# Seam between a long convolution and a GLU: last turns read from PSUM, first output in channel parts, seven residual additions as accumulating DMAs

## The chip, the cores and the metric

The kernel runs on one core of a Trainium2 chip. The metric is the device time of one execution in microseconds, the median of the runs. An execution's profile has a span, from its first to its last instruction, which is a little shorter than its time. All times below are microseconds unless they are marked ns. The engines are PE (TensorE), DVE (VectorE), ACT (ScalarE), POOL (GpSimd) and SP (SyncE, which issues most DMAs).

## The reference

One sequence of S = 2048 rows and D = 448 channels goes through two residual blocks, both modulated by a condition vector `c`.

```python
mod = (silu(c) @ w_mod).reshape(1, 6, 1, -1)
sa, ca, ga, sb, cb, gb = ...                      # six vectors of 448
h = layernorm(x) * (1 + ca) + sa
x = x + ga * A(h, k, v, shift_k, ssm_k, ssm_D)    # convolution block
h = layernorm(x) * (1 + cb) + sb
x = x + gb * B(h, w_gate, w_up, w_down)           # GLU block

def A(q, k, v, ...):
    kv = causal_depthwise_conv(k, shift_k, 4 taps) * v
    y  = causal_depthwise_conv(kv, ssm_k, S taps)  # by FFT of length 2S
    return q * (y + kv * ssm_D)

def B(x, w_gate, w_up, w_down):                   # F = 1792
    return (sigmoid(x @ w_gate) * (x @ w_up)) @ w_down
```

## The kernel before

**The convolution.** The long convolution is done as a transform by matmuls. Channels are split into two halves `h` of C = 224. `ak[h]` and `av[h]` (128 partitions x 32 x 224) hold the transforms of the filter and of `kv`. Between two transform stages a 32x32 turn is needed. It is made either on DVE, in place, for 28 channels at a time (`turn`, L181 to L183), or by a bounce through DRAM (`half_out`, `eight_out`, `half_in`, L336 to L345).

`stage2_v` (L306 to L325) loops over p = 8h + n, 16 iterations. In each, PE transforms a block of `av` (tile `s2v`, L316), DVE multiplies it by the filter (tile `m`, L320), and one iteration later `stage2_back` (L327 to L334) has PE transform it back (tile `sa`, L333) and ACT copy it from PSUM to `av` (L334). After each iteration the function `beside` (L664 to L704) adds the work of other parts that is to stand there: turns by the table `TURNS` (L660), the second transform of the filter (`stage2_k`, PE and an ACT copy, tag "y"), the modulation vectors (`mod_load` on SP, `mod_parts` and `mod_sum` on PE with an ACT copy behind each), loads, the statistics of the first layer norm, the gates (`gates`, L454: ACT and POOL prepare `gt[h, i]`), and for p from 12 on one output of the first half.

**The outputs and gates.** `stage_out(h, i)` (L347) transforms four row tiles (of 16) and one channel half to the final `y`: 16 matmuls of 224 columns into a PSUM tile (L354). `y_copy` (L357) has ACT copy it to SBUF. `gate` (L363) multiplies the prepared `gt[h, i]` by `y` (L367) and adds the product to the residual `x1` (L368). The gates of half 0 run on POOL, beside the last four iterations. Those of half 1 run on DVE: (1,0) straight from PSUM behind the loop, (1,1) to (1,3) from ACT's copies, later.

**The seam** (L706 to L725 and L903 to L924). Behind the loop come the last turn (n = 7 of half 1), the high parts of the first GLU weights (`plain_hi`, ACT) and the low remainders (`plain_lo`, DVE), modulation 5 (the gate vector of the GLU, `gbrow`), the outputs of half 1, modulation 3 (shift of the second norm, in `cols`), and the statistics of the second norm for row tiles 0 to 3 (`ln2_stats`: one tile on ACT, three on DVE; `ln2_end`: two roots on ACT, reciprocal and product on DVE). `norm_rows` (L750) normalises four row tiles into `xn`; `dup` (L758) copies 64 channels twice side by side, so that a turned tile holds them in both halves of the partitions; `norm_turn` (L765) turns them by PE into PSUM; `norm_full` (L774) has ACT apply scale and shift into `full`.

**The GLU.** All matmuls of the GLU take operands of type float32r (fp32r in the profile). Each operand is a rounded high part and a low remainder. The operand tiles of the first four "plain" quarters are "B11", "B21" (row tiles 0 to 3) and "B12", "B22" (4 to 7). `plain_half(p, q, n, f)` (L937) does 22 matmuls into tile `gu` (L944) for a weight group q, row group n and half f; the order of its 11 terms is in `OPS` or `LATE`. Then come a sigmoid (ACT, L948), a product (DVE, L949) and the split of the result (`finish_h`, L860). `down` (L873) multiplies the result by `w_down` (tile `d`, L884), and DVE adds it to `x1` (L887). The lists `turns` and `ends` (L971 to L979) say which work stands inside and behind each `plain_half`. `turn_full` (L926) makes "B12" and "B22"; it stands inside the quarter with p = 1, f = 1, its two calls after 11 and after 22 matmuls. From L1144 on 12 steps follow, of another multiplication scheme, with their side jobs in `jobs` (L1136).

**What sets the order.** The order of instructions on each engine's queue is the order in the text: `tc.manual_schedule()` (L520) keeps it. Each engine takes its own queue in that order and waits by semaphores. PSUM has 8 banks: tag "t" has two buffers of two banks, "y" and "sa" have one of two banks each; a new tile of a tag waits until the last reader of the old one is done. DMAs are issued by SP and ACT; POOL issues none.

Of the kernel before, what the change touches and what calls it, by code (L numbers as in the profile page):

```python
# [10 lines left out]
F32 = mybir.dt.float32  # L11
F32R = mybir.dt.float32r
# [67 lines left out]
def adaln_conv_glu_kernel(ctx: ExitStack, tc: tile.TileContext, q, kT, v, ssm, shift, dskip,  # L80
# [224 lines left out]

    def stage2_v(between):  # L306

        for h in range(2):
            for n in range(8):
                x, k = block(av[h], h, n), block(ak[h], h, n)  # L310
                pts = [two("t", f"s2v{h}_{n}_{b}") for b in range(2)]
                for ex in range(2):
                    for b in range(2):
                        for r in (0, 64):
                            c = r ^ 64 * b
                            PE.matmul(pts[b][c:c + 64, ex, :D], w2[r:r + 64, ex], x[r:r + 64, b], start=True, stop=True)  # L316
                m = [pairs(quad("m", 4, f"m{h}_{n}_{b}")) for b in range(2)]
                w = DT if eights(h, n) else 28
                for b in range(2):
                    DVE.tensor_mul(cols4(m[b], h, n), cols4(rows(pts[b]), h, n), k[:, b].unsqueeze(1).to_broadcast([P, 2, D // w, w]))  # L320
                products.append((h, n, m))
                if len(products) == 2:
                    stage2_back()
                between(h, n)
        stage2_back()  # L325

    def stage2_back():  # L327
        h, n, m = products.pop(0)
        pt = two("sa", f"sa{h}_{n}")
        for b in range(2):  # L330
            for ex in range(2):
                r = slice(64 * ex, 64 * ex + 64)
                PE.matmul(pt[r, b, :D], wa[:, b, r], m[b][:, ex], start=True, stop=True)  # L333
        ACT.activation(block(av[h], h, n), cols4(rows(pt), h, n), AF.Copy)  # L334
# [11 lines left out]

    def stage_out(h, i, tag):  # L347

        pt = two(tag, f"y{h}_{i}")
        for b in range(2):  # L350
            for jj in range(2):
                g = 4 * i + 2 * b + jj
                for s in range(2):
                    PE.matmul(pt[64 * s:64 * s + 64, b, jj * C:jj * C + C], wb[:, 16 * s + g], av[h][:, 16 * s + g], start=True, stop=True)  # L354
        return rows(pt)
# [7 lines left out]
    def gate(h, i, y, eng):  # L363

        gg = gt[h, i]
        xs = late["x1"][:, 4 * i:4 * i + 4, h * C:(h + 1) * C]
        eng.tensor_mul(pairs(gg), pairs(gg), y)  # L367
        eng.tensor_add(xs, xs, gg)  # L368

# [145 lines left out]

    def plain_lo(q, t):
        x = plain(q, t)
        DVE.tensor_sub(x[:, 1], ring["raw"][:, t], x[:, 0])

# [135 lines left out]
    for n in range(2):  # L655
# [5 lines left out]
             7: ((1, 4),), 8: ((1, 5),), 9: ((0, 4), (0, 5)), 10: ((0, 6), (0, 7)), 11: ((1, 6),), 12: ((1, 7),), 13: ((1, 4),),  # L661
             14: ((1, 5),), 15: ((1, 6),)}

    def beside(h, n):  # L664

        p = 8 * h + n
        for at in TURNS.get(p, ()):
            turn(av[at[0]], at[1])
        for m in {0: (0,), 1: (1,), 3: (2,), 12: (4,)}.get(p, ()):
            mod_sum(m)  # L670
        if 4 <= p < 12:
            stage2_k(1, p - 4)
        if p in (0, 2, 11):
            mod_parts({0: 1, 2: 2, 11: 4}[p], "y")
        if p == 4:
# [49 lines left out]
    y1.append(stage_out(1, 3, "sa"))  # L725
# [24 lines left out]
    def norm_rows(n, rows_=range(4)):  # L750
        for i in rows_:
            g = slice(4 * n + i, 4 * n + i + 1)
            if n == 0:
                DVE.tensor_scalar(xn[:, i], x1[:, i], rstd2[:, g], nmr2[:, g], op0=OP.mult, op1=OP.add)
            else:
                ACT.activation(xn[:, i], x1[:, 4 * n + i], AF.Identity, bias=nmr2[:, g], scale=rstd2[:, g])

    def dup():  # L758
        x = xn[:, :, P:P + 64]
        DVE.tensor_copy(xd.rearrange("p a (r c) -> p a r c", r=2), x.unsqueeze(2).to_broadcast([P, 4, 2, 64]))  # L760

# [140 lines left out]

    yc = [y_copy(1, 1, y1[1])]  # L903
# [8 lines left out]
    for t in range(2):  # L912
        norm_full(0, t, pts[0][:, t])
    for t in range(2):
        DVE.tensor_copy(xf["B11"][:, t], full[:, t])  # L915
    x_lo("B11")
    for t in range(2):
        norm_full(0, 2 + t, pts[1][:, t], xf["B21"][:, t])
    for t in range(2):
        norm_full(0, 2 + t, pts[1][:, t])  # L920
    x_lo("B21")
    ln2_stats(4, 5, 6, 7, act=(4,))
    split_plain(1, 2, 3)
# [10 lines left out]
    OPS = ((2, 0, 0, 0), (2, 1, 0, 0), (3, 0, 0, 1), (3, 1, 0, 1), (2, 0, 0, 2), (0, 0, 1, 0), (0, 1, 1, 0), (0, 0, 1, 2), (1, 0, 1, 1), (1, 1, 1, 1), (1, 0, 1, 3))  # L934
    LATE = ((2, 0, 0, 0), (2, 1, 0, 0), (3, 0, 0, 1), (3, 1, 0, 1), (0, 0, 1, 0), (0, 1, 1, 0), (1, 0, 1, 1), (1, 1, 1, 1), (2, 0, 0, 2), (0, 0, 1, 2), (1, 0, 1, 3))

    def plain_half(p, q, n, f, between=None):  # L937
        xs_ = (("B11", "B21"), ("B12", "B22"))[n]
        pt = two("t", f"gu{q}_{n}_{f}")
        ops = [(m, g) for m in range(11) for g in range(2)] if f == 0 and n == 0 else [(m, g) for g in range(2) for m in range(11)]  # L940
        order = LATE if p == f == 0 else OPS
        for i, (m, g) in enumerate(ops):
            t, s, b, k = order[m]
            PE.matmul(pt[:, g], plain(q, t)[:, s, g, f * P:f * P + P], xf[xs_[b]][:, k], start=m == 0, stop=m == 10, skip_group_check=True)  # L944
            if i in (10, 21) and between:
                between(i > 10)
# [17 lines left out]
    def form(i, k):  # L964
# [34 lines left out]
    def step(i, h, jobs):  # L999
# [131 lines left out]
        if first:  # L1131
# [3 lines left out]

    jobs = {0: {"0": [do(w_form, "A12", 4), do(w_form, "A22", 5), do(load_gu, 3, 0, 2)], "a": [do(w_form, "S4", 6)]},  # L1136
            1: {"b": [do(stats_end, 2, 3)], "c": [do(norm_rows, 2)], "e": [dup], "f": [do(turn_of, 2, 0, 1, tag="t")]},
            2: {"f": [do(turn_of, 2, 2, 3, tag="t")], "h": [do(norm_rows, 3, (0, 1))]},
            3: {"a": [do(norm_rows, 3, (2, 3))], "b": [dup], "f": [do(turn_of, 3, 0, 1, tag="t")]},
            4: {"a": [do(x_hi, "B11")], "b": [do(x_lo, "B11"), do(turn_of, 3, 2, 3)], "c": [do(t_sums, 1, 2)], "d": [do(t_sums, 3)], "e": [do(x_hi, "T2")],  # L1140
# [59 lines left out]
```

## Time and profile before

| | |
|---|---|
| median of 3 runs | 582.17 (581.55 to 583.97) |
| the profiled execution | 581.7 |
| its span | 579.9 |
| instructions | 7739 |
| PE busy | 547.4 (94% of the span) |
| DVE busy | 446.2 (77%) |
| ACT busy | 285.5 (49%) |
| POOL busy | 63.8 (11%) |
| DMA traffic | 107.72 MB, mean 186 GB/s |
| mean granted TensorE clock | 0.994 |

Busy time is the time in which an engine executes something; where PE is busy, its matmuls are pipelined and their ends are modelled. In timelines a line has the start, the time it took, the engine, the line of the kernel, the operation, output and inputs, the shape and the number of instructions merged, and in brackets the engine's idle time before it with what ended it. A view by stages has for each stretch of time the busy time of each engine (with the number of instructions), the granted clock of PE (1.00 is full), the share of the DMA engines and GB/s.

### The profile page before, as it was taken

What the parts mean: (1) busy time and instruction counts of PE and PEld (TensorE: products, weight loads), DVE (VectorE), ACT (ScalarE), POOL (GpSimd) and SP (SyncE); (2) the same over time, 40 slices, a digit from 0 to 9 for tenths busy, and PEclk for the clock granted to TensorE, in tenths of its full rate; (3) what the DMA queues carried; (4) which work ended last, traced back from release to release, by engine and by line L of the source; (5) the groups of instructions that cost most, each with busy time, mean ns of one, the idle gap of its engine ahead of it and who ended that gap; (6) DMA issues with size and microseconds to landing.
All of it is one profiled execution on the core that took longest, in us unless ns stands there. A gap on an engine that the chain in (4) does not pass through costs nothing.

```text
span 579.9 us, 7739 instructions
## 1 busy us (share of the span) xinstructions
PE 547.4 (94%) x2988; PEld 414.8 (72%) x2988; DVE 446.2 (77%) x526; ACT 285.5 (49%) x487; POOL 63.8 (11%) x54
## 2 busy tenths in 40 slices
PE   7997897899889999998999999999999999999997
PEld 6564432224457888876788888888888888888886
DVE  0899798997887868889989889886565556878564
ACT  4899495985458677346536453443121212333220
POOL 1000006978810000000000000000000000000000
PEclk9999998999989999999999999999999999999999
DMA  8999699897730224659748467567454563120103
GB/s 279 248 258 399 195 228 238 257 231 203 144 105 2 82 78 167 250 226 341 265 193 289 169 232 256 197 251 264 158 189 146 173 217 137 73 101 0 64 0 127
DMA packets 46552, 107.72 MB, mean 186 GB/s; under 512 B 19762, under 2 KB 24884, under 8 KB 45492
## 3 DMA queue, kind: packets, MB, share of 16 engines
q1 hardware_dynamic: 40212, 82.46, 47.2%
q10 hardware_dynamic: 6304, 24.78, 10.8%
q8 instruction: 23, 0.38, 0.3%
q14 instruction: 13, 0.11, 0.1%
HBM read 70.92 MB, written 35.78 MB: 184 GB/s over the span
## 4 chain that ended last, share of the span: by engine, by line
PE 75%; ACT 8%; DMA 8%; DVE 5%; issue 2%; SPq 2%; DVEq 0%; ACTq 0%
PE d L884 22%; PE b L853 15%; PE a L853 10%; PE c L853 9%; PE gu L944 6%; DMA ak<-kdk 3%; PE sa L333 2%; PE s2v L316 2%; PE y L354 2%; PE s2k L285 2%; DMA kdk<-ak 1%; SPq L195 1%; DMA inb<-in_wgu_dram 1%; DMA inb<-in_ssm_dram 1%; PE pt L771 1%
## 5 line engine op out<-in xcount | busy, mean ns | idle before, releaser
L884 PE MATMUL d<-wd,h 128*128 128x448 f32 x672 | 145.6, 366 | 2.1 <-DVE x L887 1.4
L884 PEld LDWEIGHTS d<-wd,h 128*128 128x128 f32 x672 | 125.8, 188 | 15.6 <-DVE x L887 1.8
L853 PE MATMUL b<-xt,ring 128*128 128x512 f32 x408 | 99.6, 392 | 1.1 <-DVE st L1067 0.9
L853 PEld LDWEIGHTS b<-xt,ring 128*128 128x128 f32 x408 | 76.1, 188 | 16.5 <-issue 1.3
L887 DVE TENSOR_TENSOR x<-x,d 128x896 f32<-128x896 f32 (+1 forms) x57 | 60.7, 1068 | 19.2 <-PE d L884 19.1
L853 PE MATMUL a<-x,ring 128*128 128x512 f32 x264 | 63.8, 389 | 0.0
L853 PEld LDWEIGHTS a<-x,ring 128*128 128x128 f32 x264 | 49.6, 188 | 10.3
L862 ACT ACTIVATE h<-st 128x512 fp32r<-128x512 f32 x56 | 35.2, 629 | 33.0 <-DVE st L871 20.6
L868 ACT ACTIVATE st<-st 128x512 f32<-128x512 f32 x24 | 15.2, 633 | 73.1 <-DVE st L1109 42.2
L865 DVE TENSOR_TENSOR h<-st,h 128x512 fp32r<-128x512 f32 x56 | 38.5, 688 | 15.1 <-ACT h L862 15.1
L183 DVE STREAM_TRANSPOSE av<-av 128x896 f32<-128x896 f32 x24 | 44.6, 1888 | 4.9 <-ACT av L334 2.6
L944 PE MATMUL gu<-x,ring 128*128 128x512 f32 x176 | 42.0, 392 | 0.8 <-DVE x L915 0.5
L1088 ACT ACTIVATE st<-st 128x512 f32<-128x512 f32 x12 | 7.6, 632 | 68.1 <-DVE st L1087 68.1
L320 DVE TENSOR_TENSOR m<-s2v,ak 128x896 f32<-128x896 f32 x32 | 33.4, 1089 | 7.1 <-PE s2v L316 4.1
L944 PEld LDWEIGHTS gu<-x,ring 128*128 128x128 f32 x176 | 32.7, 188 | 8.4 <-DVE x L915 0.7
L834 ACT ACTIVATE ring<-sum 128x512 fp32r<-128x512 f32 x28 | 17.3, 626 | 36.0 <-DVE sum L815 19.2
L853 PE MATMUL c<-x,ring 128*128 128x512 f32 x144 | 34.7, 390 | 0.0
L316 PE MATMUL s2v<-av,w 64*64 64x448 f32 x256 | 32.3, 558 | 0.7 <-DVE av L183 0.5
L853 PEld LDWEIGHTS c<-x,ring 128*128 128x128 f32 x144 | 27.0, 188 | 5.2
L333 PE MATMUL sa<-m,wa 128*64 128x448 f32 x128 | 27.5, 551 | 2.6 <-ACT av L334 2.6
L853 PE MATMUL c<-xt,ring 128*128 128x512 f32 x120 | 29.1, 389 | 0.0
L871 DVE TENSOR_TENSOR st<-st 128x512 f32<-128x512 f32 x24 | 16.6, 691 | 12.5 <-ACT st L868 12.4
(161 smaller groups left out, 780.7 us busy)
## 6 DMA issues: line engine op xcount, KB each, us to landing
fd<-ring ACTq DMA_DIRECT2D x35, 512.0 KB, 3.7
ring<-fd SPq DMA_DIRECT2D x35, 512.0 KB, 3.4
wdk<-wd ACTq DMA_DIRECT2D x7, 896.0 KB, 3.6
wd<-wdk SPq DMA_DIRECT2D x7, 896.0 KB, 4.5
inb<-in_wgu_dram SPq DMA_DIRECT2D x6, 1024.0 KB, 6.0
kdk<-ak SPq DMA_DIRECT2D x4, 896.0 KB, 9.9
x<-in_q_dram SPq DMA_DIRECT2D x4, 896.0 KB, 12.5
ak<-kdk SPq DMA_DIRECT2D x4, 896.0 KB, 16.7
```

The source lines that it names most:

```text
L183: DVE.transpose(x, x)
L316: PE.matmul(pts[b][c:c + 64, ex, :D], w2[r:r + 64, ex], x[r:r + 64, b], start=True, stop=True)
L320: DVE.tensor_mul(cols4(m[b], h, n), cols4(rows(pts[b]), h, n), k[:, b].unsqueeze(1).to_broadcast([P, 2, D // w, w]))
L333: PE.matmul(pt[r, b, :D], wa[:, b, r], m[b][:, ex], start=True, stop=True)
L834: ACT.activation(forms[name, i][:, 0], w_src(name), AF.Copy)
L853: PE.matmul(pt, wh(s, t), x[:, k], start=start and m == 0, stop=stop and m == len(ops) - 1, skip_group_check=True)
L862: ACT.activation(hh, h, AF.Copy)
L865: DVE.tensor_sub(hl, h, hh)
L871: DVE.tensor_mul(y[:, 0], y[:, 0], y[:, 1])
L884: PE.matmul(pt[:, i, :D], h[:, (2 * e + i) * P:(2 * e + i + 1) * P], x, start=m == 0, stop=m == len(ops) - 1)
L887: DVE.tensor_add(y, y, rows(pt)[:, a:b])
L944: PE.matmul(pt[:, g], plain(q, t)[:, s, g, f * P:f * P + P], xf[xs_[b]][:, k], start=m == 0, stop=m == 10, skip_group_check=True)
```

## The change

1. **Last two blocks of `stage2_back` (h = 1, n = 6 and 7).** PE writes the block into PSUM with 28 channels in every 32, and DVE's transpose reads PSUM and writes `av`. ACT's copy and the turn in place go. For n = 7 the PSUM tile has tag "t".
2. **Modulations and first-half outputs earlier.** `mod_parts(4)` at p = 10, `mod_sum(4)`, `mod_load(5)` and the first of the four outputs of half 0 at p = 11, `mod_parts(5)` at p = 14 (tag "y" for "sa"), `mod_sum(5)` at p = 15.
3. **First GLU weights.** `mod_load(3)`, three of the four `plain_hi` and their `plain_lo` stand ahead of the last `stage2_back`; these `plain_lo` are on POOL. `gate_wd(0)` is on DVE.
4. **Output (1,0) in two channel parts**, 196 and 28 of 224 columns, each with its own PSUM tile; the gate and the add are split likewise.
5. **Residual additions.** Of the eight gates only (1,0) adds on an engine. The other seven issue from POOL a DMA that adds `gt` to `x1`.
6. **Second norm, row tiles 0 to 3.** ACT's copy of y(1,1) stands between the two roots. Three rows are normalised on DVE, one on ACT. The duplicate copy goes; the tile of 64 channels is turned by four transposes and four matmuls with the identity. DVE writes the first two high parts straight from PSUM; their copy in `full` is made later by ACT.
7. **Behind it.** Weights 0 and 1 of group q = 1 are split before the statistics of row tiles 4 to 7. `norm_rows(1)` and `dup` stand behind the first half of the first quarter instead of its second, with the odd rows on DVE; the first turns of row group 1 stand inside p = 1, f = 0. Orders of terms change (`LATE`, `OPS1`), and more first halves interleave gate and up.
8. **Late duplicates** of row groups 2 and 3 are on ACT instead of DVE. The space for POOL's DMA descriptors is 2048 instead of 1024.

```diff
-    def stage2_v(between):
+    def stage2_v(between, last):
...
+        last()
         stage2_back()
...
     def stage2_back():
         h, n, m = products.pop(0)
-        pt = two("sa", f"sa{h}_{n}")
+        straight = h and n > 5
+        pt = two("t" if h and n == 7 else "sa", f"sa{h}_{n}")
...
-                PE.matmul(pt[r, b, :D], wa[:, b, r], m[b][:, ex], start=True, stop=True)
+                y = pt[r, b, :D] if not straight else pt[r, b].rearrange("p (j c) -> p j c", c=32)[:, :, :28]
+                PE.matmul(y, wa[:, b, r], m[b][:, ex], start=True, stop=True)
+        if straight:
+            y = pt.rearrange("p b (j c) -> p (b j) c", c=32)[:, :, :28]
+            DVE.transpose(av[h][:, :, 28 * n:28 * n + 28].rearrange("q p c -> q c p"), y.rearrange("q p c -> q c p"))
+            return
...
-        eng.tensor_add(xs, xs, gg)
+        if (h, i) == (1, 0):
+            eng.tensor_add(xs, xs, gg)
+        else:
+            POOL.dma_start(xs, gg, accum_op=OP.add)
...
-    def ln2_end(i0, n_act=2):
+    def ln2_end(i0, n_act=2, between=None):
         for i, j, w in ((i0, i0 + n_act, 1.0 / D), (i0 + n_act, i0 + 4, 1.0)):
+            if i > i0 and between:
+                between()
...
-        for m in {0: (0,), 1: (1,), 3: (2,), 12: (4,)}.get(p, ()):
+        for m in {0: (0,), 1: (1,), 3: (2,), 11: (4,), 15: (5,)}.get(p, ()):
             mod_sum(m)
...
-        if p in (0, 2, 11):
-            mod_parts({0: 1, 2: 2, 11: 4}[p], "y")
+        if p in (0, 2, 10):
+            mod_parts({0: 1, 2: 2, 10: 4}[p], "y")
...
-        if p == 12:
+        if p == 11:
             mod_load(5)
...
-        if p >= 12:
-            gate(0, p - 12, y_copy(0, p - 12, stage_out(0, p - 12, "y")), POOL)
-
-    stage2_v(beside)
-    mod_load(3)
-    turn(av[1], 7)
-    ring["k1"] = big.tile([P, 7168], F32R, tag="k1", name="ring")
-    for t in (2, 3, 0, 1):
-        plain_hi(0, t)
-    mod_parts(5, "sa")
-    y1 = [stage_out(1, 0, "t")]
-    mod_sum(5)
-    gate_wd(0)
-    for t in (2, 3, 0, 1):
-        plain_lo(0, t)
-    gate(1, 0, y1[0], DVE)
-    y1.append(stage_out(1, 1, "t"))
+        if 11 <= p < 15:
+            gate(0, p - 11, y_copy(0, p - 11, stage_out(0, p - 11, "y")), POOL)
+        if p == 14:
+            mod_parts(5, "y")
+
+    def first_forms():
+        mod_load(3)
+        ring["k1"] = big.tile([P, 7168], F32R, tag="k1", name="ring")
+        for t in (2, 0, 1):
+            plain_hi(0, t)
+        for t in (2, 0, 1):
+            plain_lo(0, t, POOL)
+
+    stage2_v(beside, first_forms)
+    plain_hi(0, 3)
+    parts = slice(0, 7 * 28), slice(7 * 28, C)
+    y10 = [stage_out(1, 0, "t", parts[0])]
+    mod_parts(3, "sa")
+    gate_wd(0, DVE)
+    y10.append(stage_out(1, 0, "t", parts[1]))
+    four = lambda x, c: pairs(x).rearrange("p b (j c) -> p b j c", c=C)[:, :, :, c]
+    for c, y in zip(parts, y10):
+        gg = four(gt[1, 0], c)
+        DVE.tensor_mul(gg, gg, y.rearrange("p b (j c) -> p b j c", c=C)[:, :, :, c])
+    for c in parts:
+        xs_ = late["x1"][:, 0:4, C + c.start:C + c.stop]
+        DVE.tensor_add(xs_, xs_, gt[1, 0][:, :, c])
+    mod_sum(3)
+    yc = []
+    y1 = [None, stage_out(1, 1, "y")]
+    y1.append(stage_out(1, 2, "t"))
     ln2_stats(0, 1, 2, 3, act=(0,))
-    mod_parts(3, "sa")
-    y1.append(stage_out(1, 2, "y"))
-    ln2_end(0, 1)
-    mod_sum(3)
+    load_gu(1, 0, 2)
+    ln2_end(0, 1, lambda: yc.append(y_copy(1, 1, y1[1])))
     y1.append(stage_out(1, 3, "sa"))
...
-            if n == 0:
-                DVE.tensor_scalar(xn[:, i], x1[:, i], rstd2[:, g], nmr2[:, g], op0=OP.mult, op1=OP.add)
+            if n == 0 and i < 3 or n == 1 and i % 2:
+                DVE.tensor_scalar(xn[:, i], x1[:, 4 * n + i], rstd2[:, g], nmr2[:, g], op0=OP.mult, op1=OP.add)
...
+    load_wd(1, wdraw)
+    norm_rows(0)
+    yc.append(y_copy(1, 2, y1[2]))
+    yc.append(y_copy(1, 3, y1[3]))
+    def norm_hi(t, y, out):
+        DVE.tensor_scalar(out, y, cols[:, t:t + 1], cols[:, 5 + t:6 + t], op0=OP.mult, op1=OP.add)
+    def turn_one(t, pt):
+        at, w = AT[t]
+        for i in range(4):
+            PE.transpose(pt[0:w, i * P:(i + 1) * P], xn[:, i, at:at + w], ident)
+            if w < P:
+                PE.matmul(pt[w:P, i * P:(i + 1) * P], xn[:, i, at:at + w], ident, start=True, stop=True)
+    p0, p2 = [ps.tile([P, 512], F32, tag="t", bufs=2, name=f"pt_{t}") for t in (0, 2)]
+    turn_one(0, p0)
+    turn_one(2, p2)
+    p13 = two("sa", "pt_13")
+    norm_hi(0, p0, xf["B11"][:, 0])
+    norm_hi(2, p2, xf["B21"][:, 0])
+    plain_lo(0, 3)
     load_gu(1, 2, 4)
-    load_gu(1, 0, 2)
-    load_wd(1, wdraw)
-    yc += [y_copy(1, i, y1[i]) for i in (2, 3)]
-    norm_rows(0)
-    dup()
-    pts = [norm_turn((0, 1), "t"), norm_turn((2, 3), "y")]
     gate(1, 1, yc[0], DVE)
...
+    norm_full(0, 0, p0)
+    turn_one(1, p13[:, 0])
+    turn_one(3, p13[:, 1])
+    norm_full(0, 1, p13[:, 0])
+    norm_full(0, 3, p13[:, 1])
+    norm_full(0, 2, p2)
+    DVE.tensor_copy(xf["B11"][:, 1], full[:, 1])
+    DVE.tensor_copy(xf["B21"][:, 1], full[:, 3])
     x_lo("B11")
...
     x_lo("B21")
+    split_plain(1, 0, 1)
     ln2_stats(4, 5, 6, 7, act=(4,))
     split_plain(1, 2, 3)
     ln2_end(4, 1)
...
-    turns = {(1, 1): lambda up: turn_full(1, 2, 3) if up else turn_full(1, 0, 1)}
-    ends = {(0, 0): [do(split_wd_hi, 0, 0), do(split_plain, 1, 0, 1)],
-            (0, 1): [do(split_wd_lo, 0, 0), do(norm_rows, 1), do(gate, 1, 2, yc[1], DVE), dup, do(gate_wd, 1, DVE)],
+    turns = {(1, 0): do(turn_full, 1, 0, 1), (1, 1): do(turn_full, 1, 2, 3)}
+    ends = {(0, 0): [do(split_wd_hi, 0, 0), do(norm_rows, 1), do(dup, DVE)],
+            (0, 1): [do(split_wd_lo, 0, 0), do(gate_wd, 1, DVE), do(gate, 1, 2, yc[1], DVE)],
```

More of the change, by code (lines that the diff above doesn't have):

```diff
@@ L345, in half_in, with stage_out @@
             nc.sync.dma_start(a[32 * b:32 * b + 32, :, c], x[b, :, :, c])
-    def stage_out(h, i, tag):
-        pt = two(tag, f"y{h}_{i}")
+    def stage_out(h, i, tag, cs=slice(0, C), pt=None):
+        pt = two(tag, f"y{h}_{i}") if pt is None else pt
         for b in range(2):
@@ L353, in stage_out @@
                 for s in range(2):
-                    PE.matmul(pt[64 * s:64 * s + 64, b, jj * C:jj * C + C], wb[:, 16 * s + g], av[h][:, 16 * s + g], start=True, stop=True)
+                    PE.matmul(pt[64 * s:64 * s + 64, b, jj * C + cs.start:jj * C + cs.stop], wb[:, 16 * s + g], av[h][:, 16 * s + g, cs], start=True, stop=True)
         return rows(pt)
@@ L514, in plain_hi, with plain_lo @@
         ACT.activation(plain(q, t)[:, 0], ring["raw"][:, t], AF.Copy)
-    def plain_lo(q, t):
+    def plain_lo(q, t, eng=DVE):
         x = plain(q, t)
-        DVE.tensor_sub(x[:, 1], ring["raw"][:, t], x[:, 0])
+        eng.tensor_sub(x[:, 1], ring["raw"][:, t], x[:, 0])
     ordered = tc.manual_schedule()
@@ L752, in norm_rows, with dup @@
             g = slice(4 * n + i, 4 * n + i + 1)
[L753 to L754 removed]
+            if n == 0 and i < 3 or n == 1 and i % 2:
+                DVE.tensor_scalar(xn[:, i], x1[:, 4 * n + i], rstd2[:, g], nmr2[:, g], op0=OP.mult, op1=OP.add)
             else:
                 ACT.activation(xn[:, i], x1[:, 4 * n + i], AF.Identity, bias=nmr2[:, g], scale=rstd2[:, g])
[L758 to L760 removed]
+    def dup(eng):
+        o, x = xd.rearrange("p a (r c) -> p a r c", r=2), xn[:, :, P:P + 64].unsqueeze(2).to_broadcast([P, 4, 2, 64])
+        if eng is ACT:
+            ACT.activation(o, x, AF.Copy)
+        else:
+            eng.tensor_copy(o, x)
     turned = []
@@ L934, in adaln_conv_glu_kernel @@
     OPS = ((2, 0, 0, 0), (2, 1, 0, 0), (3, 0, 0, 1), (3, 1, 0, 1), (2, 0, 0, 2), (0, 0, 1, 0), (0, 1, 1, 0), (0, 0, 1, 2), (1, 0, 1, 1), (1, 1, 1, 1), (1, 0, 1, 3))
-    LATE = ((2, 0, 0, 0), (2, 1, 0, 0), (3, 0, 0, 1), (3, 1, 0, 1), (0, 0, 1, 0), (0, 1, 1, 0), (1, 0, 1, 1), (1, 1, 1, 1), (2, 0, 0, 2), (0, 0, 1, 2), (1, 0, 1, 3))
+    OPS1 = tuple(x for x in OPS if x[0] < 2) + tuple(x for x in OPS if x[0] > 1)
+    LATE = ((2, 0, 0, 0), (2, 1, 0, 0), (0, 0, 1, 0), (0, 1, 1, 0), (1, 0, 1, 1), (1, 1, 1, 1), (3, 0, 0, 1), (3, 1, 0, 1), (2, 0, 0, 2), (0, 0, 1, 2), (1, 0, 1, 3))
     def plain_half(p, q, n, f, between=None):
         xs_ = (("B11", "B21"), ("B12", "B22"))[n]
-        pt = two("t", f"gu{q}_{n}_{f}")
-        ops = [(m, g) for m in range(11) for g in range(2)] if f == 0 and n == 0 else [(m, g) for g in range(2) for m in range(11)]
-        order = LATE if p == f == 0 else OPS
+        pt = two("t" if p or f else "y", f"gu{q}_{n}_{f}")
+        ops = [(m, g) for m in range(11) for g in range(2)] if p in (0, 1, 2) and f == 0 else [(m, g) for g in range(2) for m in range(11)]
+        order = LATE if p == f == 0 else OPS1 if p == 1 and f == 0 else OPS
         for i, (m, g) in enumerate(ops):
@@ L944, in plain_half @@
             PE.matmul(pt[:, g], plain(q, t)[:, s, g, f * P:f * P + P], xf[xs_[b]][:, k], start=m == 0, stop=m == 10, skip_group_check=True)
-            if i in (10, 21) and between:
-                between(i > 10)
+            if i == 10 and between:
+                between()
         sg = st[p % 2 * 2][:, f]
```

17 lines of the change are left out of this document (4 added, 13 removed).

## The prediction

> **What bounds the kernel now.** I read the busy time by stage first, then PE's timeline in the one stage where PE is not full, then what DVE and POOL do there. The stages (us from the span's start; columns: PE, PE weight loads, DVE, ACT, POOL busy, granted clock, DMA share, GB/s):
>
> ```profile
> 130.00:175.00 45.00, 39.12 (x339) 20.18 (x332) 36.31 (x41) 23.29 (x39) 28.07 (x14) 0.96 0.60 150
> 175.00:205.00 30.00, 29.58 (x139) 24.44 (x140) 22.90 (x34) 21.53 (x38) 0.00 (x0) 1.00 0.18 66
> 205.00:580.00 375.00, 366.21 (x1691) 313.83 (x1689) 280.91 (x345) 140.64 (x230) 0.00 (x0) 1.00 0.48 174
> 153.90:157.30 3.40, 2.02 (x22) 0.56 (x18) 2.31 (x2) 2.82 (x5) 2.77 (x3) 1.00 0.31 94
> 164.10:167.50 3.40, 1.89 (x24) 1.36 (x20) 2.79 (x9) 2.34 (x7) 0.00 (x0) 1.00 0.13 48
> 167.50:170.90 3.40, 3.12 (x20) 1.71 (x16) 3.23 (x7) 1.79 (x3) 0.00 (x0) 0.50 0.01 2
> ```
>
> From 205 us on PE is busy 366.21 of 375 us, so whatever is saved before that moves the rest forward unchanged. The change lies in the first two stages. PE is idle there for 45.00 - 39.12 = 5.9 us and 0.4 us. The last row adds a second loss: after a stretch with 1.89 us of work, much of it one-column matmuls, the clock is 0.50 for 3.4 us; after one with 2.02 us of full matmuls it stayed at 1.00. PE's timeline at the end of the convolution (in brackets the idle time before a group):
>
> ```profile
> 148.55 1.74 PE L316 MATMUL s2v<-av,w 64*64 64x448 f32 x16
> 150.22 1.72 PE L333 MATMUL sa<-m,wa 128*64 128x448 f32 x8
> 151.77 1.68 PE L354 MATMUL y<-av,wb 128*64 128x224 f32 x16
> 153.28 1.67 PE L333 MATMUL sa<-m,wa 128*64 128x448 f32 x8
> 155.97 0.96 PE L391 MATMUL mod<-wm,scb 112*32 112x224 f32 x16 [1.02 <-ACT av L334]
> 157.99 1.73 PE L354 MATMUL y<-av,wb 128*64 128x224 f32 x16 [1.05 <-DVE av L183]
> 159.66 1.02 PE L401 MATMUL mod<-part,ones 128*128 128x448 f32 x2
> 160.61 1.73 PE L354 MATMUL y<-av,wb 128*64 128x224 f32 x16
> 162.27 0.96 PE L391 MATMUL mod<-wm,scb 112*32 112x224 f32 x16
> 163.16 1.74 PE L354 MATMUL y<-av,wb 128*64 128x224 f32 x16
> 166.41 0.83 PE L411 MATMUL mod<-ones,part 128*128 128x1 f32 x6 [1.51 <-ACT part L394]
> 167.17 0.40 PE L414 MATMUL mod<-ones,part 128*64 128x1 f32 x8
> 167.85 3.21 PE L354 MATMUL y<-av,wb 128*64 128x224 f32 x16 [0.28 <-ACT cols L415]
> 170.99 1.97 PE L771 MATMUL pt<-ident,xn 128*128 128x128 f32 x16
> 173.47 1.20 PE L944 MATMUL gu<-x,ring 128*128 128x512 f32 x4 [0.51 <-DVE x L915]
> 174.86 14.35 PE L944 MATMUL gu<-x,ring 128*128 128x512 f32 x62 [0.20 <-DVE x L787]
> ```
>
> Idle from 155 us: 1.02 + 1.05 + 1.51 + 0.28 + 0.51 + 0.20 = 4.6 us. The output matmuls at 167.85 take 3.21 where 1.73 is normal (the half clock). DVE and POOL beside it:
>
> ```profile
> 155.96 1.98 DVE L183 STREAM_TRANSPOSE av<-av 128x896 f32<-128x896 f32 x1 [1.09 <-ACT av L334]
> 157.83 3.30 DVE L518 TENSOR_TENSOR ring<-tmp,ring 128x512 fp32r<-128x512 f32 x4
> 161.06 1.07 DVE L367 TENSOR_TENSOR inb<-inb,y 128x896 f32<-128x896 f32 x1
> 162.16 2.21 DVE L368 TENSOR_TENSOR x<-x,inb 128x896 f32<-128x896 f32 x1
> ...
> 167.63 1.78 DVE L754 TENSOR_SCALAR xn<-x,rstd,nmr 128x448 f32<-128x448 f32 x4
> ```
>
> ```profile
> 161.34 2.09 POOL L488 TENSOR_TENSOR tmp<-tmp,gbrow 128x896 f32<-128x896 f32 x1 [2.56 <-ACT gbrow L406]
> ```
>
> The chain to the first GLU matmul is: last turn, y(1,0), four weight remainders, gate, add (ends 164.37), statistics, normalised rows (from 167.63), turns, casts, 173.47. The add takes 2.21 against 1.07 for the gate: it starts as POOL's L488 runs (to 163.43) and ends 0.94 after it, so it stood still until POOL was done.
>
> **The change, step by step.** Numbers below are us on this trace's clock.
>
> *Up to the last `sa`.* Output (0,i) moves one iteration up, so the four outputs are still ahead of the last `sa`; the parts and sum of modulation 5 come ahead of it too: 0.96 + 1.02, starts counted about 1.85. Each time PE writes a tile of tag "y" right after another one, it waits for an ACT copy, as in the row at 155.97: about 1.0. There are three such waits now (parts 4 behind `s2k`, y(0,0) behind `s2k`, parts 5 behind y(0,3)) and a small one of 0.3 (as at 167.85) behind `cols`; before there were one like it and one of 0.28. That is +2.0. The next `s2v` stands behind each, and DVE behind that. The last `sa` so ends not at 153.28 + 1.67 = 154.95 but at 154.95 + 1.85 + 2.0 = 158.8.
>
> *The last turn and y(1,0).* DVE turns straight from PSUM; ACT's copy and its wait (1.09) go. The trace shows no turn out of PSUM. Bounds: 1.07 (the gate, which reads as many elements from PSUM) and 2.21 (DVE's longest such row); I take 1.98, the same operation. Turn 6 lies beside PE's sum 5 and last `sa`. Turn 7 ends at 160.8. PE meanwhile does the first 196 of 224 columns (158.8 to 160.3) and parts 3 (to 161.2). The 28 columns left cost 16 matmuls: between 0.8 (twice the 0.40 for eight one-column ones) and 1.73; I take 0.8, since they are short: 162.0. The modulation 3 load is free to start when `sa` of n=6 is done, about 156.2:
>
> ```profile
> 151.23 1.08 SPq L380 DMA_DIRECT2D wm<-in_wmod_dram  x2
> ```
>
> Here it was issued by 152.3 and used at 162.27, so it needs 10 at most; PE's 161.2 for parts 3 leaves 5. If late, PE stands still us for us, beyond a slack of 0.8 (DVE's own queue below).
>
> *Gate (1,0).* The four remainders (3.30) leave DVE: three go to POOL, one behind the turns. `gate_wd` comes to DVE (1.07): 161.9. Gate in parts 0.95 + 0.2, add 0.95 + 0.2: 164.2, against 164.37. DVE thus gains almost nothing; what is gained is that PE has its outputs behind this chain: sum 3 (1.23) to 163.2, then y(1,1), y(1,2), y(1,3) at 1.65 each to 168.15, at full clock.
>
> *To the first GLU matmul.* Add to normalised rows took 167.63 - 164.37 = 3.26; 164.2 + 3.26 = 167.45, and 0.15 more as ACT copies y(1,1) between the two roots. Three rows on DVE at 0.445: 168.95. The bank for turn 0 waits for ACT's copy of y(1,2): 169.25. Sixteen turns took 1.97; turns 0 and 2 take half: 170.3. The duplicate copy goes; turn 1 becomes four turns and four matmuls of 64 columns (bounds 0.5 and 1.73; I take 1.1, eight turns), turn 3 0.5: PE is free at 171.9. DVE writes the first high parts from PSUM in 0.65 each beside that, ready at 171.2. So the GLU starts at **171.9 instead of 173.47**, with 0.15 of waiting later instead of 0.20. The 66 matmuls at 14.35/62 = 0.2315 take 15.3: they end at 187.3 instead of 174.86 + 14.35 = 189.2. **Saved: 1.9.**
>
> *Behind it.* The order of PE from there to the third quarter, before:
>
> ```profile
> 189.21 2.43 PE d L884 x12
> 191.64 2.53 PE gu L944 x11
> 194.17 0.89 PE pt L771 x8
> ...
> 206.87 1.21 PE d L884 x6
> ```
>
> The stretch of 17.66 holds two `d` (4.86), 44 `gu` (eleven in 2.53: 10.1) and twice eight turns (0.89 and, after the row at 170.99, 1.0: 1.9) = 16.9, so 0.8 of waiting. The change sets the first eight turns 22 + 11 `gu` earlier, at 171.9 + 0.15 + 55 x 0.2315 = 184.8. They need ACT's and DVE's rows of tile group 1:
>
> ```profile
> 187.25 2.71 ACT L756 ACTIVATE xn<-x,nmr,rstd 128x448 f32<-128x448 f32 x4
> ```
>
> These were behind the second half's sigmoid and cast (2.06) and two high parts (1.04), which now come after or before; only two rows stay on ACT (1.35): 187.25 - 3.1 + 1.35 = 185.5, if the statistics of tiles 4 to 7 start at 177.5, as they did. DVE's queue (casts, remainders, two splits) gives 177.5 again. PE then waits 0.7 in place of 0.8. **Saved: 0.1.**
>
> *The accumulating DMAs.* Four adds leave POOL, three DVE; neither is the bound at their places, so that is worth nothing by itself. What is new is a wait: ACT's and DVE's statistics of tiles 4 to 7 stand behind the landing of (1,1), and behind them in ACT's queue the first sigmoid and the rows above. Its gate ends at about 172.9. The nearest rows, and one of short lines:
>
> ```profile
> av<-kd SPq DMA_DIRECT2D x8, 448.0 KB, 7.7
> ...
> wdraw<-in_wd_dram SPq DMA_DIRECT2D x6, 448.0 KB, 3.4
> ```
>
> I take 3.4 plus 0.5 to issue: 176.8, just before 177.5. Below, it could be free; above, 7.7 + 0.5 gives 181.1. Each us past 177.5 costs PE one. (1,2) and (1,3) are needed over 10 us after their gates.
>
> *Edits at nothing.* The earlier load of modulation 5 passes the bounce of the eighths on SP, whose queue is otherwise in the same order; the GLU load for q=1 waits for POOL's remainders instead of DVE's, with 10 us to spare. The two duplicates on ACT (0.6 each) lie where PE is full. On POOL the first four accumulations stand behind their gates, where the adds stood, and ahead of the remainders with 3 us of idle time between; the last three have nothing behind them. The new orders of terms only serve the first matmuls. The descriptor space and the strided `sa` write have no row; I see no work for either.
>
> **Sum**: -1.9 - 0.1 = -2.0. The profiled execution took 581.7 (span 579.9 and 1.8 around it): 579.7. The median of the runs shown, 582.17, is 0.47 above, so **580.2**.
>
> **Rivals.** *The accumulation lands late.* It has to read its target as well as its source; at twice 3.4 it lands at 172.9 + 0.5 + 6.8 = 180.2, 2.7 past 177.5: 580.2 + 2.7 = **582.9**, slower than before. It decides from 6.6 us after the gate (179.5). For it: the trace has no such DMA. Against it: the DMA share is low there (0.18).
>
> *POOL holds DVE's port, and the clock follows.* POOL's third remainder (512/896 x 2.09 = 1.2 each, from about 158.5) begins within 0.2 us of DVE's `gate_wd`. If POOL is first, `gate_wd` waits up to 1.15, as the add did at 162.16. PE's gap before the turns grows from 1.1 to 2.25, and 1.15 of 3.4 busy is less than the 1.89 that preceded the half clock: another 1.6, half of 3.2. 580.2 + 1.15 + 1.6 = **583.0**, slower. It decides from 0.85 of waiting if the clock falls too.
> The Trainium skill, "SBUF — State Buffer", section "Who interferes with whom", has the same rule for a VectorE instruction with two SBUF inputs beside a GpSimd one that reads SBUF; the row of 2.21 agrees. Its page "TensorE: Matmul & The Clock Gate", section "Why this matters for your kernels", lets the clock fall only after gaps of about 3 us; by that this rival would be 581.4. The trace differs: its longest gap here was 1.51 and the clock fell to 0.50.
>
> *Everything is earlier.* Turns out of PSUM at the lower bound (1.07) save 0.9 on the chain, and the rows of group 1 in time save the 0.7: 580.2 - 1.6 = **578.6**.
>
> **How the numbers follow.** Forecast case 0.45 (its own spread 578.8 to 581.8: six estimated sizes of some 0.5 each), late landing 0.20, port and clock 0.15, everything earlier 0.20. A measurement of this kernel can tell about 0.5%, 2.9 us, from no change. Faster by that (under 579.3): three quarters of the last case and a fifth of the forecast case, 0.25. Slower (over 585.1): landing past 183, or both bad cases at once, 0.12. Within: 0.63. The range holds the slower rivals and the fast one: 577.6 to 584.2.
>
> **What would show it.** First GLU matmul near 171.9, no half clock at 167 to 171, turn from PSUM near 1.98, x1 of tiles 0 to 3 complete at 164.2, `gate_wd` at 1.07 and not above 2, PE's wait before the first turns of group 1 about 0.7, (1,1) landing by 177.5. Wrong if the accumulation takes over 6 us, if the waits on tag "y" are not about 1.0 each, or if the clock falls at another place.

## The result and the profile after

The changed kernel took **590.3 us** (median of 4 runs, 587.52 to 593.8) beside 581.86 for the kernel before on the same chip: ratio 1.014, 95% interval 1.0101 to 1.018. The forecast was 580.2, its range 577.6 to 584.2: wrong by 10 us, and in sign. The profiled execution of after took 593.8 (span 592.0), the longest of the four, so the loss in its profile is some 3 us larger than that of the medians. Some executions of this study, here and below, were disturbed by something other than the kernel and are left out.

First, where the time was lost. TensorE's timelines, before and then after, at three marks: the back transform of the ninth iteration of the loop (which stands ahead of everything that was changed), the first GLU matmul, and the third group of `d`:

```profile
118.66 1.72 PE L333 MATMUL sa<-m,wa 128*64 128x448 f32 x8 [0.32 <-ACT av L334]
...
206.70 2.60 PE L884 MATMUL d<-wd,h 128*128 128x448 f32 x12
```

```profile
121.26 1.72 PE L336 MATMUL sa<-m,wa 128*64 128x448 f32 x8 [0.32 <-ACT av L341]
...
178.65 2.51 PE L941 MATMUL pt<-ident,xn 128*128 128x128 f32 x9 [4.44 <-DVE xn L778]
...
185.40 14.33 PE L988 MATMUL gu<-x,ring 128*128 128x512 f32 x55
...
218.79 2.60 PE L911 MATMUL d<-wd,h 128*128 128x448 f32 x12
```

From the third `d` to the end both take 373.2 (579.9 - 206.70; 592.0 - 218.79), as the forecast assumed. Up to the first mark after is 2.60 later, in code that the change doesn't touch (this mark lies at 116.1 to 121.3 in the ten profiles of this study), so below all is counted from that mark. From it to the first GLU matmul (173.47 before) it took 54.81 before, 53.24 by the forecast, and 64.14 after. **The loss sits in this stretch.** What VectorE and GpSimd did there, after:

```profile
163.21 1.72 DVE L339 STREAM_TRANSPOSE av<-sa 128x896 f32<-128x896 f32 x1 [0.52 <-PE sa L336]
164.75 3.46 DVE L500 TENSOR_TENSOR tmp<-tmp,gbrow 128x896 f32<-128x896 f32 x1
168.14 1.14 DVE L738 TENSOR_TENSOR inb<-inb,y 128x784 f32<-128x784 f32 x2
169.20 5.40 DVE L741 TENSOR_TENSOR x<-x,inb 128x784 f32<-128x784 f32 x2
177.99 1.36 DVE L778 TENSOR_SCALAR xn<-x,rstd,nmr 128x448 f32<-128x448 f32 x3
```

```profile
145.93 1.47 POOL L378 DMA_DIRECT2D x<-G  x1 [0.33 <-POOL G L374]
...
152.48 1.32 POOL L378 DMA_DIRECT2D x<-G  x1 [2.94 <-issue]
...
163.85 1.30 POOL L378 DMA_DIRECT2D x<-G  x1 [7.91 <-issue]
164.67 2.59 POOL L374 TENSOR_TENSOR G<-G,tmp 128x896 f32<-128x896 f32 x1
169.38 1.32 POOL L378 DMA_DIRECT2D x<-G  x1 [2.13 <-issue]
170.21 4.24 POOL L530 TENSOR_TENSOR ring<-tmp,ring 128x512 fp32r<-128x512 f32 x3
```

GpSimd stood still 2.94, 7.91 and 2.13 in front of its second, third and fourth accumulation (13.0 together). "issue" means that the profile shows nothing it waited for. The view of the DMAs has the first three landing 6.3, 11.1 and 5.2 after their issue, so at 152.2, 163.6 and 169.1, and each time the next was issued some 0.3 later. So the last gate of half 0 ran at 164.67 and the remainders at 170.21, both beside VectorE's instructions with two SBUF inputs: `gate_wd` took 3.46, ending 0.95 after the gate, and the add 5.40, ending 0.15 after the remainders. The Trainium skill, "SBUF — State Buffer", section "Who interferes with whom", says that such a VectorE instruction and a GpSimd one that reads SBUF lock each other out for a whole instruction; the row of `gate_wd` agrees. The add went further: a narrower window of the same timeline splits it into 0.96 for the first 784 elements and 4.51 for the last 112 (from 170.09), which stood still through all three remainders. Against the forecast, counted from the mark, the last turn ends 1.5 late, `gate_wd` 3.7, the add 7.8, the first GLU matmul 10.9. The 1.5 is a half clock at y(0,0), ahead of the accumulations (row of 137.40 below); the last 3.1 come from the turns, which follow a gap of 4.44 on TensorE. The view by stages shows their clock (third value from the end, 0.53):

```profile
160.00:178.00 18.00, 12.14 (x124) 7.20 (x120) 16.62 (x18) 6.09 (x15) 8.48 (x6) 1.00 0.83 170
178.00:188.00 10.00, 9.35 (x30) 6.10 (x31) 5.70 (x10) 5.33 (x8) 1.29 (x1) 0.53 0.48 111
```

Two more rows of TensorE's timeline, and the accumulations' own cost: the page's row of their queue (packets, MB, share of 16 engines), and issues with KB each and median time to landing between 140 and 192 us:

```profile
137.40 3.16 PE L361 MATMUL y<-av,wb 128*64 128x224 f32 x16 [1.04 <-ACT ak L291]
...
164.84 1.55 PE L361 MATMUL y<-av,wb 128*64 128x196 f32 x16 [1.69 <-DMA av<-kd]
```

```profile
q0 software_dynamic: 3696, 3.21, 3.8%
```

```profile
x<-G POOLq DMA_DIRECT2D x4, 448.0 KB, 5.8
av<-kd SPq DMA_DIRECT2D x4, 448.0 KB, 9.4
```

Seven accumulations held 3.8% of 592: 3.2 us of all 16 engines each, in 528 packets. And TensorE waited 1.69 for the bounce of `av` through DRAM, which it did not await before. In this profile that wait cost nothing yet: the first 196 columns of y(1,0) were done at 166.39 and the other 28 at 168.32, and VectorE, held in `gate_wd`, came to their gates only at 168.14 and 169.02.

### The profile page after: what moved, and what is told of

It is laid out like the page before. It is cut to its first block, busy times and chain, and to the rows that moved or that the text cites. A ratio compares the mean times of both kernels' runs of the same rounds, so it can differ in the third digit from the quotient of the medians.

```text
span 592.0 us, 7802 instructions
## 1 busy us (share of the span) xinstructions
PE 555.3 (94%) x3012; PEld 419.1 (71%) x3012; DVE 447.5 (76%) x523; ACT 283.2 (48%) x484; POOL 66.4 (11%) x59
## 4 chain that ended last, share of the span: by engine, by line
PE 65%; DVE 2%; DMA 1%; ACT 1%; issue 0%; DVEq 0%; ACTq 0%
PE d L911 22%; PE b L880 15%; PE a L880 10%; PE c L880 9%; PE gu L988 7%; DMA inb<-in_wgu_dram 1%; PE pt L798 1%; PE pt L941 1%; PE pt L943 0%; DVE ring L865 0%; ACT ring L861 0%; DVE st L1153 0%; ACT st L1077 0%; DVE st L1111 0%; ACT h L889 0%
## 5 line engine op out<-in xcount | busy, mean ns | idle before, releaser
L988 PE MATMUL gu<-x,ring 128*128 128x512 f32 x176 | 43.2, 402 | 0.0
L183 DVE STREAM_TRANSPOSE av<-av 128x896 f32<-128x896 f32 x22 | 40.6, 1874 | 3.3 <-ACT av L232 2.3
L988 PEld LDWEIGHTS gu<-x,ring 128*128 128x128 f32 x176 | 34.0, 195 | 7.0
```

The costliest lines, as they stand in the source:

```text
L183: DVE.transpose(x, x)
```

## The experiments

Theories. **A**: GpSimd's queue stands still until the accumulation before has left the small descriptor space; its compute falls late, on VectorE's instructions. **B**: the accumulations share the DMA engines with the bounce that TensorE awaits. **C**: the waits on tag "y" and the clock, nothing of the DMAs. Per run the median, then the ratio to before with its interval; in the table the time from the mark.

| kernel | first GLU matmul | third `d` | ratio |
|---|---|---|---|
| before | 54.81 | 88.04 | 1 |
| after | 64.14 | 97.53 | 1.0140 |
| more descriptor space | 63.80 | 97.08 | 1.0163 |
| half-0 adds on GpSimd | 53.98 | 87.34 | 1.0014 |
| no accumulation | 53.98 | 87.27 | 1.0013 |
| before + four accumulations | 58.39 | 91.89 | 1.0067 |
| accumulations later | 53.98 | 104.23 | 1.0298 |
| accumulations behind the remainders | 54.00 | 87.87 | 1.0016 |
| no accumulation, turn 1 by copy | 52.05 | 86.72 | 1.0015 |
| parts ahead | 49.63 | 84.53 | 0.9960 |
| parts ahead, `gate_wd` between the turns | no usable profile | | 0.9927 |

**More descriptor space** (4096 bytes; to make room, two rows share a tile with a later sum):

```diff
-dynamic_dma_scratch_size=2048
+dynamic_dma_scratch_size=4096
```

> The changed kernel with 4096 instead of 2048 bytes of descriptor space for POOL's DMAs (one table of weight sums moves into the dead arow and brow to make room). Theory A (POOL's queue stands still until the accumulation before has left the descriptor space, so that POOL's later work falls on DVE's two-operand work): POOL's standstills of 2.9, 7.9 and 2.1 us before its issues shrink to under 1 each, gate_wd on DVE takes about 1.1 instead of 3.5, the add of gate (1,0) at most 2.5 instead of 5.4, and the time falls to 580 to 584. Theory B (the accumulations slow the bounce through DRAM, whose landing PE awaits): standstills may shrink, but PE still waits 1.7 for the bounce and the time stays at 587 to 591. Theory C (waits on tag y and the clock falls, nothing to do with POOL): 588 to 591.

592.11 us, 1.0163 (1.0106 to 1.0219). GpSimd's timeline: no accumulation of half 0 waits over 0.36 us now. VectorE and TensorE:

```profile
163.26 1.37 DVE L500 TENSOR_TENSOR tmp<-tmp,gbrow 128x896 f32<-128x896 f32 x1
...
173.84 1.15 DVE L741 TENSOR_TENSOR x<-x,inb 128x784 f32<-128x784 f32 x2
```

```profile
168.07 2.88 PE L361 MATMUL y<-av,wb 128*64 128x196 f32 x16 [6.43 <-DMA av<-kd]
```

The standstill was the descriptor space: with more of it, it is gone, and so are the long `gate_wd` and add. But the time that A foresaw did not come: the accumulations now overlap beside the bounce (issued 4 to 5 us apart, landing after 10.7 in the median), TensorE's wait for it grows from 1.69 to 6.43, the outputs behind it run at the half clock (2.88 for 1.55), and the first GLU matmul comes no sooner. The loss changed its place. The Trainium skill, "DMA: Bandwidth & Descriptors", section "Queues, rings and completion order", lets each DMA engine take turns between the queues packet by packet; a bounce that lands later the more accumulations run beside it agrees.

**The half-0 adds back on GpSimd**, the three late accumulations kept; and **no accumulation**, all else of the change kept:

```diff
-        if (h, i) == (1, 0):
+        if h == 0 or i == 0:
             eng.tensor_add(xs, xs, gg)
```

```diff
-            POOL.dma_start(xs, gg, accum_op=OP.add)
+            eng.tensor_add(xs, xs, gg)
```

> The changed kernel with the four adds of half 0 on POOL again (2.1 us each); the three late ones stay accumulating DMAs. Theory A: POOL has no standstill, its remainders run from about 159 to 164, gate_wd may still lose up to 1.2 to them and the add up to 1; time 581 to 585. Theory B: the bounce lands 5 us earlier than in the changed kernel and PE's wait of 1.7 for it goes; time 586 to 589 if that is all. Theory C: 588 to 591.

> The changed kernel with all seven adds on the engines (POOL for half 0, DVE for half 1). If only the accumulations of half 0 cost (theories A and B), within 0.4% of the run with the four adds on POOL. If the late three cost too, faster than that by 1 us or more; if they help, slower by about 1 (three DVE adds of 1.1 beside the first matmuls of the GLU). Theory C: 588 to 591.

583.14 (1.0014, 0.9982 to 1.0045) and 583.13 (1.0013, 0.9989 to 1.0038). So the four half-0 accumulations carry the whole loss, 7.2 us by the medians, the late three nothing that could be measured, and C falls. The rest of the change is worth nothing that could be measured, where -2.0 was forecast. The first of the two shows the stretch without the loss (VectorE, GpSimd, then TensorE):

```profile
158.97 1.80 DVE L339 STREAM_TRANSPOSE av<-sa 128x896 f32<-128x896 f32 x1 [0.50 <-PE sa L336]
160.63 1.29 DVE L500 TENSOR_TENSOR tmp<-tmp,gbrow 128x896 f32<-128x896 f32 x1
161.84 1.14 DVE L738 TENSOR_TENSOR inb<-inb,y 128x784 f32<-128x784 f32 x2
162.90 1.16 DVE L741 TENSOR_TENSOR x<-x,inb 128x784 f32<-128x784 f32 x2
```

```profile
158.45 4.60 POOL L530 TENSOR_TENSOR ring<-tmp,ring 128x512 fp32r<-128x512 f32 x3 [0.56 <-ACT ring L526]
```

```profile
168.13 2.04 PE L941 MATMUL pt<-ident,xn 128*128 128x128 f32 x9 [0.34 <-DVE xn L778]
170.09 0.43 PE L943 MATMUL pt<-ident,xn 128*64 128x128 f32 x2
170.46 0.30 PE L941 MATMUL pt<-ident,xn 128*64 128x128 f32 x1
...
172.65 13.53 PE L988 MATMUL gu<-x,ring 128*128 128x512 f32 x55
```

Here too `gate_wd` runs beside GpSimd's remainders, and it takes only 1.29. This time GpSimd waited: its third remainder took 2.12, the first two 1.28 each. So it is not the meeting that costs, but which of the two has to wait. Counted from the mark against this kernel, after lost 1.57 up to the end of the last turn (the half clock at y(0,0)), 2.13 in `gate_wd`, 4.24 up to the end of the add and 2.22 up to the first GLU matmul: the 10.16 of the table.

**Before, plus the four accumulations** (descriptor space 2048):

```diff
+        if h:
             eng.tensor_add(xs, xs, gg)
+        else:
+            POOL.dma_start(xs, gg, accum_op=OP.add)
```

> The kernel before with the four adds of half 0 as accumulating DMAs (descriptor space 2048), nothing else changed. There POOL has only gate_wd behind them (2.1, needed late). Theory A: POOL is held again for 5 to 15 us in all and gate_wd on POOL moves back by 5 to 12 us, onto DVE's statistics and normalised rows, where it can hold two-operand or two-port work for up to 2.1; time 582 to 586. Theory B: the bounce lands 5 us later, at about 156.5, still ahead of its use at 158, so at most 1 to 2 us. Theory C: within 0.3% of the kernel before.

585.8, 1.0067 (1.0041 to 1.0093). TensorE doesn't await the bounce here, so this is A by itself, in the old order: standstills of 8.51, 2.20 and 4.58 on GpSimd, and on VectorE

```profile
164.84 3.18 DVE L369 TENSOR_TENSOR x<-x,inb 128x896 f32<-128x896 f32 x1
...
171.73 4.87 DVE L757 TENSOR_SCALAR xn<-x,rstd,nmr 128x448 f32<-128x448 f32 x4 [0.58 <-PE mod L417]
```

where before had 2.21 and 1.78. The second row overlaps GpSimd's late `gate_wd` (from 172.47) and its last issue of an accumulation (171.64 to 172.95). Its instructions have one SBUF input only; the section "Who interferes with whom" of the Trainium skill, named above, lists `tensor_scalar` among the operations that can take the shared ports too. The sixteen turns behind it took 4.55 for 1.97, at a granted clock of 0.50 from 172 to 180: here, too, the clock adds to A.

**Accumulations later.** (0,0) at once, (0,1) behind the remainders, (0,2) and (0,3) behind the accumulation of (1,1):

```diff
+        elif h == 0 and i:
+            held_acc.append((xs, gg))
...
+            plain_lo(0, t, POOL)
+        acc_now(1)
...
     gate(1, 1, yc[0], DVE)
+    acc_now(2)
```

> The changed kernel with its seven accumulating DMAs, but three of the four of half 0 issued later: (0,0) at once, (0,1) behind POOL's remainders, (0,2) and (0,3) behind the accumulation of gate (1,1). Theory A plus B (POOL's queue stands still behind an accumulation, and the accumulations slow the bounce through DRAM that TensorE awaits): with both places freed the gates (0,1) to (0,3) and the remainders come without a standstill, the part of (1,0) on VectorE without a held gate_wd and add, so the time is that of the kernel with the half-0 adds on POOL: 583 us (582 to 585). Were the mere presence of the DMAs the cost (their bytes on the 16 engines, wherever they stand), it stays at 587 to 591. Theory C (waits on tag y and the clock, nothing to do with POOL): 590.

599.75, 1.0298 (1.0264 to 1.0332): worse than any, and none of the three theories' numbers. The waits of SP and of TensorE say why:

```profile
SPq L504 <- DMA x<-G: 26.5, 1, 26.5
```

```profile
PE pt L807 <- ACT xn L789: 15.6, 1, 15.6
```

A load of `w_down` overwrites the buffer that the accumulations read. It waited on SP for them, and the load of GLU weights behind it kept ScalarE, and so TensorE. Up to the first GLU matmul all was as A and B foresaw (`gate_wd` 1.30, add 1.16, no wait for the bounce), but the time says nothing of them. So, mended: **accumulations behind the remainders**, that load behind the load of GLU weights, the add of (1,1) on VectorE:

```diff
-        acc_now(1)
+        acc_now(3)
...
     load_gu(1, 2, 4)
+    load_wd(1, wdraw)
     gate(1, 1, yc[0], DVE)
-    acc_now(2)
```

> As the run before with accumulations issued later, whose 599.75 us came from a load: wd(1) overwrites the buffer that the accumulations of (0,2) and (0,3) read, so the load waited 26.5 us on SP for them, and the load of gu(1) behind it came 19 us late. Here (0,1), (0,2) and (0,3) are issued back to back behind POOL's remainders, the load of wd(1) stands behind that of gu(1), and the add of (1,1) is on VectorE; six accumulations remain (0,0 at once). Theory A plus B: no standstill of POOL ahead of work that VectorE or TensorE needs and no wait of TensorE for the bounce, so 583 us (582 to 585), that of the kernels with the half-0 adds on POOL or with no accumulation. If accumulations cost by their bytes or their presence wherever they stand, 587 or more. The load of gu(1) now runs beside two accumulations: if that load lands over 4 us later than 175, the next wait is there and the time is 585 to 587.

582.47, 1.0016 (0.999 to 1.0042). Six accumulations remain, GpSimd still stands still:

```profile
164.09 1.32 POOL L384 DMA_DIRECT2D x<-G  x1
170.50 1.29 POOL L384 DMA_DIRECT2D x<-G  x1 [5.09 <-issue]
176.57 1.30 POOL L384 DMA_DIRECT2D x<-G  x1 [4.78 <-issue]
```

but nothing is queued behind it that anyone needs, and TensorE doesn't wait for the bounce. Place, not presence or bytes, was the cost.

**Turn 1 by a doubled copy**, no accumulation:

```diff
+    dup(DVE)
...
-            PE.transpose(pt[0:w, i * P:(i + 1) * P], xn[:, i, at:at + w], ident)
-            if w < P:
-                PE.matmul(pt[w:P, i * P:(i + 1) * P], xn[:, i, at:at + w], ident, start=True, stop=True)
+            PE.transpose(pt[:, i * P:(i + 1) * P], xn[:, i, at:at + P] if w == P else xd[:, i], ident)
```

> All adds on engines, and turn 1 of the opening by four transposes of a doubled copy (made by VectorE) in place of four transposes and eight one-row-block identity matmuls. In the kernels of the change turn 1 took 2.2 us and not the 1.1 of the prediction. If that is what ate the gain of the opening, turn 1 falls to about 0.55, the copy costs VectorE about 0.3 to 0.5 beside TensorE's first two turns, and the time is 581.5 us (1.6 under the kernel without accumulations, 583.1). If the turns stand beside something that ends later, it stays at 583.

582.41, 1.0015 (0.9988 to 1.0043): no gain that could be measured. TensorE:

```profile
169.76 2.82 PE L939 MATMUL pt<-ident,xn 128*128 128x128 f32 x16 [0.45 <-DVE xn L775]
172.34 2.09 PE L984 MATMUL gu<-x,ring 128*128 128x512 f32 x8
175.97 11.24 PE L984 MATMUL gu<-x,ring 128*128 128x512 f32 x47 [1.54 <-DVE x L957]
```

The turns are 1.7 shorter (2.82 for 4.52), but the ninth GLU matmul waits 1.54 for VectorE's cast. At the third `d` 0.55 is left.

**Parts ahead**: half-0 adds on GpSimd, turn 1 by the copy, and modulation parts 4 and 5 and y(0,0) put between `s2v` and `sa` of their step, so that the waits on tag "y" pass under the other matmuls; `gate_wd` behind gate (1,1). The core of it:

```diff
-        if 11 <= p < 15:
+        if 12 <= p < 15:
...
+    def ahead(p):
+        if p in (11, 15):
+            mod_parts({11: 4, 15: 5}[p], "y")
+        if p == 12:
+            gate(0, 0, y_copy(0, 0, stage_out(0, 0, "y")), POOL)
```

> Half-0 adds on POOL, the three late accumulations kept, turn 1 by the doubled copy, and the matmuls of modulation parts 4, y(0,0) and parts 5 placed between the products and the back turn of their step, where the three waits of about 1.0 us each on tag y go; gate_wd of half 0 stands on VectorE behind gate (1,1). If these waits are on the path that sets the end: 3.0 less for the waits and 1.6 less for turn 1 than the 583.1 of the kernel with the half-0 adds on POOL, 578.5 us (577 to 580), under both kernels. If the waits only move to the copies of ScalarE behind them: 581.5.

578.96, 0.996 (0.9937 to 0.9983): faster than before, the first here. The three waits are gone and the first GLU matmul comes 4.35 sooner than with the half-0 adds on GpSimd alone; 1.78 is given back at the ninth GLU matmul, where VectorE's cast stands behind `gate_wd`. And the add of (1,0) is drawn out again, without any accumulation near it: 3.02 for 1.16, beside GpSimd's remainders (VectorE, then GpSimd):

```profile
156.10 3.02 DVE L745 TENSOR_TENSOR x<-x,inb 128x784 f32<-128x784 f32 x2
```

```profile
154.51 4.47 POOL L531 TENSOR_TENSOR ring<-tmp,ring 128x512 fp32r<-128x512 f32 x3
```

Because of the 1.78, `gate_wd` was moved **between the two turns**:

```diff
             plain_lo(0, t, POOL)
+        gate_wd(0, DVE)
```

> The kernel with the parts ahead (578.96 us), with gate_wd of half 0 moved from behind gate (1,1), where VectorE was 1.78 us late for TensorE's third pair of ring matmuls, to between the two turns from PSUM, where VectorE had 0.84 us of idle time. If that gate_wd was what made TensorE wait: 0.8 less (1.1 off the wait, 0.3 put on the last turn), 578.1 us (577 to 579.3). If VectorE's casts are late for another reason: 579 to 579.5.

0.9927 (0.9901 to 0.9953), from four runs of 576.63 to 580.29: 4.2 us under before. The intervals of the two kernels overlap, and there is no usable profile of this one, so that the 1.78 was `gate_wd`'s fault is not shown: with turn 1 by the copy and no accumulation, TensorE waited 1.54 at the same place with another VectorE instruction there, the add of (1,1).

## Why the prediction was wrong

The step that failed is in "Edits at nothing": "On POOL the first four accumulations stand behind their gates, where the adds stood, and ahead of the remainders with 3 us of idle time between", with "that is worth nothing by itself" ahead of it. It took an accumulation to cost GpSimd no more than the add that it replaces, and the instructions behind it nothing. The runs showed 13.0 us of standstill on GpSimd (A) and a bounce that is delayed (B); together +7.2 us by the medians, taken away by taking away the four half-0 accumulations, or by putting three of them behind the remainders. In after's own profile, apart from the 1.57 ahead of all accumulations, A alone decided, through `gate_wd`, the add and the clock of the turns; B took its place once A was removed. The line "The descriptor space and the strided `sa` write have no row; I see no work for either" named the cause of the standstill and passed it by: a resource with no row was set to nothing, not bounded from both sides.

Point by point:

- *Waits on tag "y"*: right, three of about 1.0 and one of 0.3; moving them, with turn 1 by the copy and `gate_wd` later, was worth 2.8 at the third `d`.
- *Last turn from PSUM*: 1.72 to 1.82 for 1.98; `gate_wd` 1.29 for 1.07; the parts 1.14 and 1.16 for 1.15 each. Right where VectorE does not have to wait for GpSimd.
- *First GLU matmul 1.57 earlier*: 0.83 in the kernels without the half-0 accumulations. With the half-0 adds on GpSimd, turns 0 and 2 were done at about 169.8 (forecast 170.3, at nearly the same mark), but turn 1 took about 2.3 for 1.1 (from about 169.9 to 172.2: pairs of 0.43 and single turns of 0.30). That term was mis-sized by 1.2, past the upper bound given (1.73). And its size decided little, as the copy showed: the cast was next.
- *-2.0 in all*: -0.7 at the third `d`, +0.8 (-0.6 to +2.2) by the medians. What stands between the two stays open; the stretch up to the mark, untouched, varies by more.
- *Rival "the accumulation lands late"*: refuted as a cost. (1,1) took 4.9 to 5.2 from its issue, between the 3.9 of the forecast and the 7.3 of the rival. With the half-0 adds on GpSimd it landed at 178.0 for the 177.5 allowed, and ScalarE waited 1.96 for it; TensorE's wait before the first turns of group 1 was 0.21 with it and 0.21 without any accumulation.
- *Rival "POOL holds DVE's port, and the clock follows"*: the right mechanism, port and half clock both, at the right instruction. It was priced for GpSimd without a standstill, 1.15 + 1.6, and there it hardly showed (`gate_wd` 1.29 for 1.07, the clock stayed up); with GpSimd 13 us late it struck twice, for 6.3 on VectorE and some 2.2 on the turns.
- *The half clock at y(0,0)* stands in two of the ten profiles, those of after and of after with more descriptor space, ahead of all accumulations. Its cause stays open, and so does whether some of the 7.2 is due to it.

## What to carry to other kernels

In these kernels an accumulating DMA stood in GpSimd's queue until the one before it had landed, and everything behind it stood with it: ask what stands behind each issue, and place several of them where nothing follows. Giving them more room only moved the loss, to the bounce that shared the DMA engines at that time. And moving the last reader of a buffer later moves every load that overwrites it, and all that is queued behind that load.

## What the runs showed of the hardware that was not expected

In the profile of after, an accumulating DMA of 448 KB took GpSimd 1.3 us to issue, held all 16 engines for 3.2 and landed after 4.9 to 11.1 (median 5.2). With 2048 bytes of descriptor space, one that came while another was under way was issued only when that had landed, after 2.1 to 8.5 us of standstill in the four kernels that had it; with 4096 no accumulation of half 0 waited over 0.36. A VectorE row of `TENSOR_SCALAR` with one SBUF input was drawn out too, from 1.78 to 4.87 for four, beside a GpSimd instruction and the issue of an accumulation. And a turn out of PSUM took 1.72 to 1.82, a little less than most within SBUF (1.76 to 2.01 in the same profiles, medians 1.87 to 1.91).
